# Linear attention and a tanh-shrink MLP on one core: the denominator of batches 3 to 7 taken from TensorE, a DRAM round trip and VectorE to GpSimd and VectorE

## The chip, the cores and the metric

The kernel runs on one core of one Trainium2 chip. The metric is the device time of one execution in microseconds (us), the median of three: 287.32 before (287.25 to 287.70). The profile is of one execution more, with its own time.

## The reference, cut to what matters

```python
# q, k, v: [8 batches, 8 heads, 576, 64] f32
phi = lambda x: np.where(x > 0, x, np.exp(x) - 1.0) + 1.0
kv  = einsum('bhsd,bhse->bhde', phi(k), v)
z   = sum(phi(k), axis=2)
num = einsum('bhsd,bhde->bhse', phi(q), kv)
den = einsum('bhsd,bhd->bhs', phi(q), z)[..., None] + 1e-6
x   = (num / den).transpose(0, 2, 1, 3).reshape(4608, 512)
h   = x @ w_in                  # w_in [512, 2048]
out = (h - tanh(h)) @ w_out     # w_out [2048, 512]
```

Each batch gives 576 rows of x; the MLP takes them in nine blocks of 512 rows.

## The kernel before

Everything is in one hand-written order. A loop of nine passes (`for c in range(NC)`, L509) does the MLP on rows 512c to 512c+511. A pass has two halves of 16 slots each. In **layer 1** a slot is one fi of 16: four matmuls (`l1mm`, L366) of w_in with xT, the transposed x in bf16, into bank fi % 6 of PSUM. After every second slot ScalarE takes tanh of two banks (`l1act2`, L372) and VectorE subtracts, which gives gT in bf16 (L373). In **layer 2** a slot is a quarter of one of four output tiles: four matmuls (`l2mm`, L387) into bank 4 or 5. After slots 3, 7, 11 and 15 ScalarE copies the finished tile to osb (`evac`, L396) and SP writes it out (L403). The dictionaries `s1` and `s2` hold what is put in after a slot: the attention of the batches that later passes need. An engine runs its instructions in the order in which they were written, so a waiting one holds all behind it.

Batches 0 and 1 and part of 2 are prepared in their own way at the start. In the steady part, pass c (c >= 1) with n1 = c + 1 and n2 = c + 2 does this:

- Layer 1, slot 0: `gate` (L383), a copy of one element of qT(n1) on GpSimd, which waits for the transposing DMA; behind it, in GpSimd's queue, the loads of k, q and v of batch n2 (L90), cast to bf16 on the way.
- Layer 1, slot 8 (10 in pass 1): `a_den(n1)`. 16 matmuls (L287) of kz and qT give den for 32 x 4 partitions, in which eight heads and four 16-row groups are folded; kz holds kv in its columns 0 to 63 and, in 64 to 95, z times a mask (L199). VectorE adds 1e-6 (L292) and takes the reciprocal (L296). Then `a_spread(n1)`: SP writes rden to DRAM (four DMAs, L316) and reads it back spread over 64 partitions each (two DMAs, L319) as rdb.
- Layer 2, slots 2, 4, 6 and 8: phi of k (two halves) and of q (two halves): the exponential on ScalarE (L129), max and add (L130) and the minimum (L131) on VectorE. After slot 8 SP issues the transposing DMA (L148), which makes qT(n2) from phi(q). Slots 3 and 5: `a_vp` copies v(n2) beside columns of ones (L190), so that the kv matmuls give z too.
- Layer 2, slot 9 (12 in pass 1): `a_num(n1, n2)`: the num matmuls (L228, and L236 for the last 64 rows), the kv matmuls of batch n2 (L177), then VectorE multiplies num by rdb from PSUM into xT (L333 four times, L338 twice), then `kz_copy(n2)` takes z and kv of batch n2 out of banks 6 and 7 (L199, L200).

The row names in the profile are those of this text. The prediction numbers times within a pass from the start of layer 1 (U) and of layer 2 (T). Other rows that it prices by: L159, transposes of phi(q) on TensorE for batches 0 and 1; L163, L244, L525, ScalarE's copies out of PSUM there; L359, a multiplication of VectorE there; L421, a memset on GpSimd; the select of `masks.py:199`, on GpSimd; L503, a sum of eight elements on VectorE. The kv matmuls of pass 1 that belong to batch 2 stand at its layer 1, slot 8.

Of the kernel before, what the change touches and what calls it, by code (L numbers as in the profile page):

```python
# [11 lines left out]
F32 = mybir.dt.float32  # L12
# [6 lines left out]
def kernel(  # L19
# [15 lines left out]
    NF = DF // 128  # L35
    NC = N // 512
    J = S // 64


    const = ctx.enter_context(tc.tile_pool(name="const", bufs=1))  # L40
# [71 lines left out]


    kp_t, qp_t, qT_t, kz_t, rdb_t, rden_t = {}, {}, {}, {}, {}, {}

    def phi_pieces(b, src, store, name, i, parts=0):

# [71 lines left out]
    def a_vp(b, i):  # L189
        nc.vector.tensor_copy(vp[:, i, :, :, 0:64].rearrange("p j h d -> p h j d"), v_b[b % 2][:, 0:2, i])  # L190

    def kv_cols_mm(b, b0, o):
        kz_t[b] = kz_c[b % 2]
        kv_mm(b, lambda rs, h, i, j: vp[rs, i, j, h, :],
              lambda cs, hg, i: ps_all[cs, b0 + hg, o + 66 * i:o + 66 * i + 66])

    def kz_copy(b, b0, o):
        ps = ps_all[:, b0:b0 + 2, o:o + 132].rearrange("p g (i e) -> p g i e", i=2)
        nc.vector.tensor_mul(kz_t[b][:, :, :, 64:96], ps[:, :, :, 64:65].to_broadcast([128, 2, 2, 32]), mask)  # L199
        nc.vector.tensor_copy(kz_t[b][:, :, :, 0:64], ps[:, :, :, 0:64])  # L200


    def b0_z(i):
# [74 lines left out]
    def a_den(b, bank, parts=range(4)):  # L278

        kz, qT = kz_t[b], qT_t[b]  # L280
        ps = ps_all[:, bank, 0:J * 16]
        for t in range(4) if b == 0 else ():
            nc.tensor.matmul(ps[32 * t:32 * t + 32], eps[:, 0:32], one[:, 0:J * 16], start=True, stop=False)
        for n, p in enumerate((0, 2, 1, 3)):
            if n in parts:
                for t in range(4):
                    nc.tensor.matmul(ps[32 * t:32 * t + 32], kz[:, p // 2, p % 2, 64:96],  # L287
                                     qT[:, p % 2, :, p // 2, 16 * t:16 * t + 16],
                                     start=(n == 0 and b > 0), stop=(n == NP - 1))
        if b > 0:  # L290
            den = rpool.tile([128, J * 16], F32, name="den")
            nc.vector.tensor_scalar(den, ps, 1e-6, None, ALU.add)  # L292
        else:
            den = ps
        rden = rpool.tile([128, J * 16], F32, name="rden")
        nc.vector.reciprocal(rden, den)  # L296
        rden_t[b] = rden
# [25 lines left out]

    def a_num(b, nxt):

        rdb = rdb_t[b]
        for i in range(2):
            num_mm(b, i, lambda h: 2 * h + i)
        rest = rest_mm(b, 6, 0)
        if nxt:  # L330
            kv_cols_mm(nxt, 6, 128)
        for n in range(NP):
            nc.vector.tensor_mul(  # L333
                xT[:, n, S * b:S * b + 512].rearrange("p (j t c) -> p j t c", j=8, t=4),
                ps_all[:, n, :].rearrange("p (j t c) -> p j t c", j=8, t=4),
                rdb[:, n, :, 0:8, :].rearrange("p t j c -> p j t c"))
        for h in range(2):
            nc.vector.tensor_mul(  # L338
                xT[:, 2 * h:2 * h + 2, S * b + 512:S * b + 576].rearrange("p a (t c) -> p a t c", t=4),
                rest[h].rearrange("p a (t c) -> p a t c", t=4), rdb[:, 2 * h:2 * h + 2, :, 8, :])  # L340
        if nxt:
            kz_copy(nxt, 6, 128)

    def new_ns(b):

# [34 lines left out]
    def gate(qT):  # L380

        g0 = rpool.tile([1, 1], BF16, name="g0")
        nc.gpsimd.tensor_copy(g0, qT[0:1, 1, J - 1, 1, 63:64])  # L383
# [6 lines left out]
    def evac(c, i, o, f0=0, f1=None):  # L390
        f1 = DM if f1 is None else f1
        osb = opool.tile([128, DM], F32, name="osb")
        if f0:
            nc.vector.tensor_copy(osb[:, f0:f1], o[:, f0:f1])  # L394
        else:
            nc.scalar.copy(osb[:, f0:f1], o[:, f0:f1])  # L396

        last = c == NC - 1 and i == 3
        for half in range(2):
            b, j = divmod(2 * (4 * c + i) + half, J)  # L400
            cuts = [f0, 256, f1] if c == 3 and i < 3 else [f0, f1]
            for a0, a1 in zip(cuts, cuts[1:]):
                (nc.scalar if last and half else nc.sync).dma_start(  # L403
                    out=out[b * S:(b + 1) * S, a0:a1].rearrange("(p j) m -> p j m", j=J)[:, j, :],
                    in_=osb[64 * half:64 * half + 64, a0:a1])
# [103 lines left out]
    for c in range(NC):  # L509
# [4 lines left out]
        if c == 0:  # L514
            sub = {}

            def spread1(h):
                sub["bp"] = a_spread_pe(1, 4, (2 * h, 2 * h + 1))
                for p in (2 * h, 2 * h + 1):
                    a_scale(1, p, sub["ns"], sub["bp"], 144 * (p % 2))  # L520

            def num1():
                ns = sub["ns"] = new_ns(1)
                for h, ps in enumerate(rest_mm(1, 6, 128)):
                    nc.scalar.copy(ns[:, 2 * h:2 * h + 2, 8, :], ps)  # L525
                for i in range(2):
                    b0 = 4 + 2 * i
                    num_mm(1, i, lambda h: b0 + h)
                    nc.scalar.copy(ns[:, i::2, 0:8, :].rearrange("p a j t -> p a (j t)"), ps_all[:, b0:b0 + 2, :])

            s1[11].append(lambda: a_kphi(1, 0))
            s1[13].append(lambda: a_kphi(1, 1))
            s2[3].append(lambda: a_qphi(1, 0))
            s2[4].append(lambda: (a_qphi(1, 1), load_q(2), load_k(2), load_v(2)))
            s2[0].append(prepare)
            s2[7].append(lambda: (a_qT_pe(1, 0, Banks([4, 5])), a_kv(1, 6), a_qT_pe(1, 1, Banks([4, 5]))))
            s2[8].append(lambda: (scale_rest(0, 6, rdb_t[0]), a_den(1, 4), num1(), a_split(1)))
            s2[10].append(lambda: spread1(0))

            qs, ks = [], []  # L540

            def exp2(pieces, src, store, name, i):
                pieces.append(phi_pieces(2, src, store, name, i))
                pieces[i][0]()

            def rest2(f):
                f[1]()
                f[2]()

            s2[11].append(lambda: exp2(qs, q_t, qp_t, "qp", 0))  # L550
            s2[12].append(lambda: (spread1(1), exp2(qs, q_t, qp_t, "qp", 1), rest2(qs[0])))
            s2[13].append(lambda: (exp2(ks, k_t, kp_t, "kp", 0), rest2(qs[1]), a_qT_dma(2)))
            s2[14].append(lambda: rest2(ks[0]))
        elif n1 < B:
            if c == 1:
                s1[8].append(lambda: (kv_cols_mm(2, 6, 0), kz_copy(2, 6, 0)))
            s1[10 if c == 1 else 8].append(lambda: (a_den(n1, 6), a_spread(n1)))
            s2[12 if c == 1 else 9].append(lambda: a_num(n1, n2 if n2 < B else 0))
        if c == 1:
            s1[1].append(lambda: a_kphi(2, 1))  # L560
            s1[3].append(lambda: (a_vp(2, 0), a_vp(2, 1)))
        if c >= 1 and n2 < B:

            s1[0].append(lambda: (gate(qT_t[n1]), load_k(n2), load_q(n2), load_v(n2)))
            d = 2
            s2[d].append(lambda: a_kphi(n2, 0))
            s2[d + 2].append(lambda: a_kphi(n2, 1))
            s2[d + 4].append(lambda: a_qphi(n2, 0))
            s2[d + 6].append(lambda: (a_qphi(n2, 1), a_qT_dma(n2)))
            for i in range(2):  # L570
                s2[d + 1 + 2 * i].append(lambda i=i: a_vp(n2, i))
        if c == 0:

            first = Banks([4, 5, 6, 7, 0, 1, 2, 3])
            hs = [ps_all[:, n, :] for n in range(4)]
            order = [((0, 0), (0, 1)), ((2, 0), (2, 1), (0, 2), (0, 3), (2, 2), (2, 3)),
                     [(p, fi) for p in (1, 3) for fi in range(4)]]
            seen = [0] * 4
            for n, part_ in enumerate(order):
                if n == 1:  # L580
                    open2()
                for x in range(2 if n == 0 else 0):
                    for p, fi in part_:
                        nc.tensor.matmul(hs[fi][:, 256 * x:256 * x + 256], w_in_sb[:, p, fi * 128:(fi + 1) * 128],
                                         xT[:, p, 256 * x:256 * x + 256], start=(x == 0), stop=False)
                        seen[fi] = 1
                for p, fi in part_ if n else ():
                    l1mm(c, fi, hs[fi], p, seen[fi])
                    seen[fi] += 1
            for fi in range(4):  # L590
                l1act(fi, hs[fi], gT)
# [74 lines left out]
```

## Time and profile before

| | |
|---|---|
| median of three runs | 287.32 us |
| profiled execution, its own time | 287.78 us |
| its span, first to last instruction | 286.0 us |
| mean granted TensorE clock | 0.998 |
| layer 1 of passes 2 to 6, each | 14.28 to 14.29 us |
| layer 1 of pass 7 | 13.81 us |
| transposing DMA, issue to landing, passes 1 to 4 | 6.86, 5.26, 5.19, 4.07 us |
| loads of k, q, v, issue to landing | 6.6, 8.6, 11.1 us |

"Busy" is the time in which an engine ran instructions. PE is TensorE, PEld its weight loads, DVE is VectorE, ACT is ScalarE, POOL is GpSimd, SP only issues DMAs. The chain that ended last is followed back from the last instruction, at each step to what released it; its pieces in order of time give the start, the length and the line. The rows by line give an operation's shape, count, mean duration, and how long its engine was idle just before it and for whom. The transposing DMA's issue is read on SP's timeline, its landing from the gate copy that waits for it.

### The profile page before, as it was taken

What the parts mean: (1) busy time and instruction counts of PE and PEld (TensorE: products, weight loads), DVE (VectorE), ACT (ScalarE), POOL (GpSimd) and SP (SyncE); (2) the same over time, 40 slices, a digit from 0 to 9 for tenths busy, and PEclk for the clock granted to TensorE, in tenths of its full rate; (3) what the DMA queues carried; (4) which work ended last, traced back from release to release, by engine and by line L of the source; (5) the groups of instructions that cost most, each with busy time, mean ns of one, the idle gap of its engine ahead of it and who ended that gap; (6) DMA issues with size and microseconds to landing.
All of it is one profiled execution on the core that took longest, in us unless ns stands there. A gap on an engine that the chain in (4) does not pass through costs nothing.

```text
span 286.0 us, 5195 instructions
## 1 busy us (share of the span) xinstructions
PE 276.8 (97%) x2127; PEld 130.8 (46%) x2155; DVE 171.3 (60%) x271; ACT 139.6 (49%) x167; POOL 30.0 (10%) x50
## 2 busy tenths in 40 slices
PE   8889999999999999999999999999999999999995
PEld 3544464444444444445444544444444444444443
DVE  3749977997558782877277727874680467006600
ACT  4848557857335643564355625661551155126411
POOL 8642030120030003000300030000000000000000
PEclk9999999999999999999999999999999999999999
DMA  6999999997979668955996679656126210230032
GB/s 98 197 206 213 208 207 208 233 179 147 235 148 207 162 102 151 222 127 132 147 208 148 145 142 216 148 126 138 39 75 138 68 37 0 52 82 16 0 76 73
DMA packets 39496, 38.99 MB, mean 136 GB/s; under 512 B 16368, under 2 KB 34608, under 8 KB 38704
## 3 DMA queue, kind: packets, MB, share of 16 engines
q0 software_dynamic: 17488, 18.35, 39.5%
q1 hardware_dynamic: 21824, 20.17, 30.8%
q8 instruction: 17, 0.28, 0.4%
q10 hardware_dynamic: 160, 0.13, 0.1%
q14 instruction: 7, 0.06, 0.1%
HBM read 43.91 MB, written 9.55 MB: 187 GB/s over the span
## 4 chain that ended last, share of the span: by engine, by line
PE 93%; DMA 2%; issue 1%; POOL 1%; DVE 1%; DVEq 0%; POOLq 0%
PE ps_all L366 43%; PE ps_all L387 42%; DMA v<-in_v_dram 2%; PE ps_all L177 2%; PE ps_all L228 1%; PE ps_all L622 1%; PE ps_all L287 1%; PE ps_all L251 1%; POOL kraw L87 1%; DVE xT L255 0%; POOL qraw L87 0%; PE ps_all L159 0%; DVE rden L296 0%; PE ps_all L236 0%; PE ps_all L354 0%
## 5 line engine op out<-in xcount | busy, mean ns | idle before, releaser
L366 PE MATMUL ps_all<-xT,w_in_sb 128*128 128x512 bf16 x559 | 125.4, 379 | 1.2 <-issue 0.5
L387 PE MATMUL ps_all<-w_out_sb,gT 128*128 128x512 bf16 x547 | 122.2, 379 | 1.3 <-issue 1.0
L373 DVE TENSOR_TENSOR gT<-ps_all,th 128x1024 bf16<-128x1024 f32 x64 | 77.8, 1217 | 66.7 <-ACT th L372 66.7
L372 ACT ACTIVATE th<-ps_all 128x1024 f32<-128x1024 f32 x64 | 65.5, 1023 | 50.1 <-PE ps_all L366 50.1
L366 PEld LDWEIGHTS <-w_in_sb 128*128 128x128 bf16 x574 | 55.4, 98 | 67.1 <-issue 0.6
L387 PEld LDWEIGHTS <-gT 128*128 128x128 bf16 x560 | 54.1, 98 | 64.4 <-issue 0.2
L396 ACT COPY osb<-ps_all 128x512 f32<-128x512 f32 (+1 forms) x36 | 20.8, 582 | 74.0 <-PE ps_all L387 49.0
L129 ACT ACTIVATE e<-qraw 128x1152 bf16<-128x1152 bf16 x16 | 18.5, 1160 | 8.4 <-DMA qraw<-in_q_dram 8.4
L333 DVE TENSOR_TENSOR xT<-ps_all,rdb 128x512 bf16<-128x512 f32 x24 | 14.9, 681 | 9.1 <-PE ps_all L228 6.7
L129 ACT ACTIVATE e<-kraw 128x1152 bf16<-128x1152 bf16 x15 | 17.4, 1161 | 0.4 <-DMA kraw<-in_k_dram 0.4
L131 DVE TENSOR_TENSOR qp<-e,r 128x1152 bf16<-128x1152 bf16 x16 | 12.1, 758 | 6.0 <-ACT e L129 5.1
L131 DVE TENSOR_TENSOR kp<-e,r 128x1152 bf16<-128x1152 bf16 x15 | 11.4, 758 | 5.9 <-ACT e L129 4.9
L383 POOL COPY g<-qT 1x1 bf16<-1x1 bf16 x5 | 0.9, 177 | 115.1 <-DMA qT<-qp 115.1
L378 DVE TENSOR_TENSOR gT<-ps_all,th 128x512 bf16<-128x512 f32 x16 | 10.3, 685 | 2.6 <-ACT th L377 2.0
L377 ACT ACTIVATE th<-ps_all 128x512 f32<-128x512 f32 x16 | 9.2, 598 | 4.9 <-PE ps_all L366 3.7
L449 PE MATMUL ps_all<-zero 128*128 128x512 bf16 x29 | 8.7, 460 | 1.2 <-DVE zero L408 1.2
L130 DVE TENSOR_SCALAR r<-qraw 128x1152 bf16<-128x1152 bf16 x16 | 7.5, 468 | 3.0 <-DMA qraw<-in_q_dram 3.0
L296 DVE RECIPROCAL rden<-den 128x144 f32<-128x144 f32 x7 | 7.4, 1053 | 0.2
L394 DVE COPY osb<-ps_all 128x128 f32<-128x128 f32 x1 | 0.3, 290 | 11.6 <-PE ps_all L622 11.6
L130 DVE TENSOR_SCALAR r<-kraw 128x1152 bf16<-128x1152 bf16 x15 | 6.8, 450 | 0.0
L90 POOL DMA_DIRECT2D qraw<-in_q_dram x7 | 5.2, 749 | 13.7 <-DVE r L130 13.0
L177 PEld LDWEIGHTS <-kp 64*64 64x64 bf16 x504 | 5.5, 105 | 0.6 <-DVE vp L190 0.4
(83 smaller groups left out, 111.9 us busy)
## 6 DMA issues: line engine op xcount, KB each, us to landing
out_dram<-osb SPq DMA_DIRECT2D x64, 128.0 KB
rdb<-ds SPq DMA_DIRECT2D x12, 576.0 KB
kraw<-in_k_dram POOLq DMA_DIRECT2D x7, 576.0 KB, 6.6
qraw<-in_q_dram POOLq DMA_DIRECT2D x7, 576.0 KB, 8.6
v<-in_v_dram POOLq DMA_DIRECT2D x7, 576.0 KB, 11.1
w_in_sb<-in_moe_w_in_dram POOLq DMA_DIRECT2D x3, 512.0 KB, 13.4
w_out_sb<-in_moe_w_out_dram POOLq DMA_DIRECT2D x3, 512.0 KB, 19.4
out_dram<-osb SPq DMA_DIRECT2D x12, 64.0 KB
```

Of the source, the lines that this page charges most:

```text
L129: return (lambda: nc.scalar.activation(e, x, AF.Exp), lambda: nc.vector.tensor_scalar(r, x, 0.0, 1.0, ALU.max, ALU.add), lambda: nc.vector ...
L130: lambda: nc.vector.tensor_scalar(r, x, 0.0, 1.0, ALU.max, ALU.add),
L131: lambda: nc.vector.tensor_tensor(y, e, r, ALU.min))
L177: nc.tensor.matmul(ps_of(cs, hg, i), kp[rs, i, j, h, :], v_of(rs, h, i, j), start=(j == 0), stop=(j == J - 1))
L333: nc.vector.tensor_mul(xT[:, n, S * b:S * b + 512].rearrange("p (j t c) -> p j t c", j=8, t=4), ps_all[:, n, :].rearrange("p (j t c) -> p ...
L366: nc.tensor.matmul(h, w_in_sb[:, p, fi * 128:(fi + 1) * 128], xT[:, p, c * 512:(c + 1) * 512], start=(n == 0), stop=(n == NP - 1))
L372: nc.scalar.activation(th, h, AF.Tanh)
L373: nc.vector.tensor_sub(gT[:, fi:fi + 2, :], h, th)
L377: nc.scalar.activation(th, h, AF.Tanh)
L378: nc.vector.tensor_sub(gT[:, fi, :], h, th)
L387: nc.tensor.matmul(o, gT[:, fi, i * 128:(i + 1) * 128], w_out_sb[:, fi, :], start=(fi == 0), stop=(fi == NF - 1))
L396: nc.scalar.copy(osb[:, f0:f1], o[:, f0:f1])
```

## The change

For batches 3 to 7 (`QS = 3`) phi(q) is divided by den before it is transposed, so that num comes out divided.

- `kz_copy` no longer makes the masked z for them; VectorE copies z from PSUM into zr, repeated 64 times along the free axis (bf16). It now stands ahead of the copies into xT, also in pass 1, where batch 2's own multiplications (`num_scale`) come behind it.
- `q_zb`, two slots after a_num: two matmuls of zr with the identity turn z into a row that is the same on all partitions; ScalarE copies it to zb.
- `q_prod`: GpSimd multiplies phi(q) by zb in two halves of 1152 elements, in f32 (the buffers of rdb are used for the products).
- `q_den`: VectorE sums 64 elements at a time, four instructions of 576 elements. Two stand after layer 2's slot 15, two in layer 1 of the next pass, after slots 3 and 5; for batch 3 all stand in layer 1 of pass 2, after slots 2, 5 and 7.
- `q_scale`, after slot 7 (9 in pass 2): VectorE adds 1e-6 and takes the reciprocal of 36 elements; GpSimd multiplies phi(q) by it in place, two halves; then SP issues the transposing DMA.
- `a_den` and `a_spread` are gone for these batches; in `a_num` VectorE copies one half of num into xT and ScalarE the other.
- The loads of batch c + 3 are issued after layer 2's slot 9 of pass c, without the gate; only pass 1 keeps its gate and its loads of batch 3 in layer 1.
- In pass 3 only the first two output tiles are written in half rows.

```diff
+    QS = 3
...
     def kz_copy(b, b0, o):
...
+        if b < QS:
+            nc.vector.tensor_mul(kz_t[b][:, :, :, 64:96], ps[:, :, :, 64:65].to_broadcast([128, 2, 2, 32]), mask)
+        else:
+            zr_t[b] = rpool.tile([128, 2, 2, 64], BF16, name="zr")
+            nc.vector.tensor_copy(zr_t[b].rearrange("p i g t -> p g i t"),
+                                  ps[:, :, :, 64:65].to_broadcast([128, 2, 2, 64]))
         nc.vector.tensor_copy(kz_t[b][:, :, :, 0:64], ps[:, :, :, 0:64])
+    def q_zb(b, bank):
+        ps = ps_all[:, bank, 0:256]
+        for i in range(2):
+            nc.tensor.matmul(ps[:, 128 * i:128 * i + 128], zr_t[b][:, i].rearrange("p g t -> p (g t)"), ident,
+                             start=True, stop=True)
+        zb_t[b] = rpool.tile([128, 2, 128], BF16, name="zb")
+        nc.scalar.copy(zb_t[b].rearrange("p i x -> p (i x)"), ps)
+    def q_prod(b):
+        pr_t[b] = rpool.tile([128, 2, J, 2, D], F32, name="pr", tag="rdb")
+        dn_t[b] = rpool.tile([128, 2, J, 2], F32, name="dn")
+        for i in range(2):
+            nc.gpsimd.tensor_mul(pr_t[b][:, i].rearrange("p j h d -> p j (h d)"),
+                                 qp_t[b][:, i].rearrange("p j h d -> p j (h d)"),
+                                 zb_t[b][:, i].unsqueeze(1).to_broadcast([128, J, 128]))
+    def q_den(b, i, h):
+        nc.vector.tensor_reduce(dn_t[b][:, i, :, h], pr_t[b][:, i, :, h, :], mybir.AxisListType.X, ALU.add)
+    def q_scale(b):
+        dn = dn_t[b].rearrange("p i j h -> p (i j h)")
+        nc.vector.tensor_scalar(dn, dn, 1e-6, None, ALU.add)
+        rd = rpool.tile([128, 2, J * 2], F32, name="rd")
+        nc.vector.reciprocal(rd.rearrange("p i x -> p (i x)"), dn)
+        for i in range(2):
+            x = qp_t[b][:, i].rearrange("p j h d -> p (j h) d")
+            nc.gpsimd.tensor_mul(x, x, rd[:, i].unsqueeze(2).to_broadcast([128, J * 2, D]))
+        a_qT_dma(b)
...
     def a_num(b, nxt):
...
+        if nxt >= QS:
+            kz_copy(nxt, 6, 128)
+        if b >= QS:
+            for h, copy in enumerate((nc.vector.tensor_copy, nc.scalar.copy)):
+                copy(xT[:, 2 * h:2 * h + 2, S * b:S * b + 512], ps_all[:, 2 * h:2 * h + 2, :])
+                copy(xT[:, 2 * h:2 * h + 2, S * b + 512:S * b + 576], rest[h])
+        else:
+            num_scale(b, rest)
...
-            cuts = [f0, 256, f1] if c == 3 and i < 3 else [f0, f1]
+            cuts = [f0, 256, f1] if c == 3 and 2 * i + half < 4 else [f0, f1]
...
-            s1[10 if c == 1 else 8].append(lambda: (a_den(n1, 6), a_spread(n1)))
-            s2[12 if c == 1 else 9].append(lambda: a_num(n1, n2 if n2 < B else 0))
+            if n1 < QS:
+                s1[10].append(lambda: (a_den(n1, 6), a_spread(n1)))
+            else:
+                if c == 2:
+                    s1[2].append(lambda: (q_den(n1, 0, 0), q_den(n1, 0, 1)))
+                e = 2 * (c == 2)
+                s1[3 + e].append(lambda: q_den(n1, 1, 0))
+                s1[5 + e].append(lambda: q_den(n1, 1, 1))
+                s1[7 + e].append(lambda: q_scale(n1))
+            m = 12 if c == 1 else 9
+            s2[m].append(lambda: a_num(n1, n2 if n2 < B else 0))
+            if n2 < B:
+                s2[m + 2].append(lambda: (q_zb(n2, 4 if c == 1 else 7), q_prod(n2)))
+                if c > 1:
+                    s2[15].append(lambda: (q_den(n2, 0, 0), q_den(n2, 0, 1)))
...
-            s1[0].append(lambda: (gate(qT_t[n1]), load_k(n2), load_q(n2), load_v(n2)))
...
-            s2[d + 6].append(lambda: (a_qphi(n2, 1), a_qT_dma(n2)))
+            s2[d + 6].append(lambda: a_qphi(n2, 1))
...
+            if n2 + 1 < B:
+                s2[9].append(lambda: (load_k(n2 + 1), load_q(n2 + 1), load_v(n2 + 1)))
```

More of the change, by code (lines that the diff above doesn't have):

```diff
@@ L114 @@
     kp_t, qp_t, qT_t, kz_t, rdb_t, rden_t = {}, {}, {}, {}, {}, {}
+    zr_t, zb_t, pr_t, dn_t = {}, {}, {}, {}
     def phi_pieces(b, src, store, name, i, parts=0):
@@ L198, in kz_copy @@
         ps = ps_all[:, b0:b0 + 2, o:o + 132].rearrange("p g (i e) -> p g i e", i=2)
-        nc.vector.tensor_mul(kz_t[b][:, :, :, 64:96], ps[:, :, :, 64:65].to_broadcast([128, 2, 2, 32]), mask)
-        nc.vector.tensor_copy(kz_t[b][:, :, :, 0:64], ps[:, :, :, 0:64])
+        if b < QS:
[4 more added lines that the diff above has]
+                                  ps[:, :, :, 64:65].to_broadcast([128, 2, 2, 64]))
+        nc.vector.tensor_copy(kz_t[b][:, :, :, 0:64], ps[:, :, :, 0:64])
+    def q_zb(b, bank):
[23 more added lines that the diff above has]
+        a_qT_dma(b)
     def b0_z(i):
@@ L324, in a_num @@
     def a_num(b, nxt):
-        rdb = rdb_t[b]
         for i in range(2):
@@ L331, in a_num, with num_scale @@
             kv_cols_mm(nxt, 6, 128)
+        if nxt >= QS:
[6 more added lines that the diff above has]
+            num_scale(b, rest)
+    def num_scale(b, rest):
+        rdb = rdb_t[b]
         for n in range(NP):
@@ L340, in a_num @@
                 rest[h].rearrange("p a (t c) -> p a t c", t=4), rdb[:, 2 * h:2 * h + 2, :, 8, :])
-        if nxt:
-            kz_copy(nxt, 6, 128)
     def new_ns(b):
@@ L561 @@
             s1[3].append(lambda: (a_vp(2, 0), a_vp(2, 1)))
+            s1[0].append(lambda: (gate(qT_t[n1]), load_k(n2), load_q(n2), load_v(n2)))
         if c >= 1 and n2 < B:
-            s1[0].append(lambda: (gate(qT_t[n1]), load_k(n2), load_q(n2), load_v(n2)))
             d = 2
```

## The prediction

> **What bounds the kernel now.** I read the busy shares first, then the chain that ended last, then its pieces in order of time, then the rows by line.
>
> ```profile
> PE 276.8 (97%) x2127; PEld 130.8 (46%) x2155; DVE 171.3 (60%) x271; ACT 139.6 (49%) x167; POOL 30.0 (10%) x50
> PEclk9999999999999999999999999999999999999999
> PE 93%; DMA 2%; issue 1%; POOL 1%; DVE 1%; DVEq 0%; POOLq 0%
> ```
>
> TensorE is busy 97% of the span, with nine tenths or more of its clock granted in every slice, and is 93% of the chain; from pass 2 on nothing else stands in that chain but small "issue" gaps. So the time changes only by work put on or taken off TensorE, and by any new wait that makes it stand. VectorE and GpSimd have room on average; whether they have it at the right moment is the question. The chain in order of time (start, length, what), for pass 3 and the last but one, pass 7:
>
> ```profile
> 139.50 5.61 PE ps_all L366 x26
> 145.17 2.11 PE ps_all L366 x9
> 147.28 0.36 PE ps_all L287 x16
> 147.64 5.29 PE ps_all L366 x24
> 152.98 0.81 PE ps_all L366 x3
> 153.79 8.63 PE ps_all L387 x40
> ...
> 227.28 5.61 PE ps_all L366 x26
> 232.94 8.15 PE ps_all L366 x37
> 241.09 2.59 PE ps_all L387 x12
> ```
>
> Layer 1 of pass 3 runs from 139.50 to 153.79: 14.29 us. Pass 7 has the same 64 matmuls and no den: 227.28 to 241.09, 13.81. So the 16 den matmuls of L287 cost 0.48, not the 0.36 of their own piece: changing to them and back costs the rest. Passes 2, 4, 5 and 6 give 14.28 in the same way. A slot (4 matmuls) is 13.81/16 = 0.863 us, in layer 1 and layer 2 alike.
>
> **TensorE, part by part.** Removed: five dens (batches 3 to 7) at 0.47: 2.35 us. Added: five times two matmuls of 128x128 (`q_zb`). Nine matmuls of that shape, the transposes at L159, take 0.50 and 0.61 in the chain, so two are 0.11 to 0.14. The change to another kind of work may cost a gap: 0.16 ("issue") stands behind the kv matmuls in most passes. Bounds 0.11 to 0.30; I take 0.20, five times: 1.0. Net 1.35 off; with the bounds 0.85 to 1.80. The num and kv matmuls stay as they are.
>
> All else must stay off TensorE's path. I check each new wait, in times from the start of layer 2 (T) or layer 1 (U) of a pass.
>
> **`q_zb` waits for VectorE and ScalarE.** It stands behind slot 11. a_num starts at T 8.6; its matmuls and kv end near T 10.1, and two slots later it is T 11.8. Before it VectorE must do zr (in the place of L199; 256 elements as in L200, 0.41) and kz (0.41), from T 10.1: done at T 10.9. ScalarE must have read bank 7: its half of the xT copies is 1024 and 128 elements, L244 1.01 and L525 0.27, from T 9.3: done at T 10.6. So about 0.9 us of cover; gone, each lost us is paid five times, by all of layer 2 queued behind.
>
> **VectorE in layer 1.** Removed per batch: den 0.30 and reciprocal 1.05. Added: four sums of 576 f32 elements. The trace has no such sum: a sum over 8 elements takes 0.16 (L503), a two-source operation on 576 f32 0.75 (L359); these are the bounds, and I take 0.70, near the upper one, since the element count sets it. Then an addition and a reciprocal on 36 elements: 0.4 (a quarter of the 144-element work, plus a little; at most 1.35). Two sums come ahead of the first gT (L373), when VectorE idles: in before it waits 5.3 us there. The other two and the scale each stand behind a gT. gT takes 1.22 of each 1.73; one sum makes a gT at most 0.3 late. TensorE needs a pair of banks again six slots after filling it, that is 5.2 us after the fill begins; tanh and gT end 4.0 after it, which leaves 1.2. With sums in between 0.8 is left, in pass 2, where both first sums fall behind the first gT, about 0.3. Cost nothing; at the 0.75 bound still nothing, or 0.1 once.
>
> **VectorE in layer 2.** Four multiplications (L333, 0.68) and two (L338, 0.28) become a copy of 1024 (L373's size, at most 1.22) and one of 128: earlier, not later. Pass 1 is different: batch 2 keeps its multiplications, but kz(3) now goes ahead of them. They start at 78.6 instead of 77.1, at 0.6 each, and the last of the four ends at 81.1; pass 2 needs it at 80.7 plus five matmuls, 81.8. Hidden by 0.7.
>
> **GpSimd and the transposing DMA, the long chain.** The change puts four two-input multiplications of 1152 elements per batch on GpSimd. No row has one. Below: a memset of the same 1152 (L421) 1.08. Above: the select on 128 elements takes 0.287, nine times that is 2.58; if two inputs were read one after the other, twice: 5.2. I take 2.6, the row nearest in kind, and call its price p.
>
> Products: zb is copied behind the osb copy of slot 11, by T 12.9 (0.37, between L525's 0.27 and L396's 0.58). GpSimd is free: the loads now put into its queue ahead (0.75 each) wait for phi(q)'s end, T 8.7, and are issued by T 10.2. Products end at T 15.5 and T 18.1; the sums that need them are due at T 15.2 (idle VectorE) and T 21. Covered until p is about 4.5.
>
> Scaling: rd is ready at U 10.1 (behind gT of fi 7) and two multiplications end at U 15.3. Then SP issues the transposing DMA; it landed 4.07, 5.19 and 5.26 us after issue in passes 4, 3 and 2 (issue on SP's timeline to the gate copy at L383), and 6.86 in pass 1. With 4.1 to 5.3 qT is there at U 19.5 to 20.7, and num needs it at U 13.8 + 8.6 = 22.4: cover 1.7 to 2.9, until p is 3.5 to 4.0. In pass 2 all is two slots later: rd at 92.7, GpSimd done at 97.9, landed at 102.1 to 103.3; num is due at 103.1. This is the thinnest place: cover 1.0, or short by 0.2. I take the shorter landing: in before the transpose follows two output copies, and in pass 3 six more follow it; now it comes some 12 us after the last output copy was issued. On SP the next output copies queue behind it; they are due at T 3.5 or later and osb has five buffers.
>
> **The loads.** In before the gate (L383) holds them until qT has landed; 11.1 us later v is in. Now they are issued 4 us before layer 1 and land about U 6 to 8, long before the next phi, and before the transpose at U 15.4. Also 30 DMAs of rden (four at L316 and two of 576 KB at L319 per batch) leave SP's queue; batch 2 keeps its six. Neither is on the chain: nothing gained.
>
> The Trainium skill speaks against this placing: "GPSIMD Engine Reference", section "Elementwise — side-by-side cycle accounting", gives two-input work about 2.6 cycles per element at 1.2 GHz. By that page 1152 elements are an estimated 2.5 us plus its dispatch, and the sum would be the same as with my row; no run here has shown it yet. "SBUF — State Buffer", section "Who interferes with whom", says that a VectorE instruction with two SBUF inputs, or in a two-port mode, and a GpSimd instruction lock each other out for a whole instruction. By that rule the second multiplication of pass 2 (to 97.9) would hold back phi(k)'s L130, due at 96.9, by 1.0 us; VectorE waits 0.88 and 0.74 for ScalarE's exponentials in that stretch, so it would cost nothing or a few tenths.
>
> **The sum.** The profiled execution took 287.78: span 286.0 and 1.78 around it. 287.78 - 2.35 + 1.0 = 286.43. It lies 0.46 above the median 287.32, so on the median: 285.97, said as **286.0**.
>
> **Rivals.**
> A, the pass 2 transpose is late: everything as above, but landing takes 5.3 to 6.9, or p is 3.3. TensorE stands 0.2 to 1.7 once, in the middle 1.0: 287.0. For it: cover 1.0 at best. Against: no output copies beside it.
> B, the gaps eat it: q_zb with two gaps and its waits costs 0.4 rather than 0.2, and 0.3 of the den comes back at num; five times 0.4: about 287.2, the change doing nothing. For it: den's 0.48 was one quarter gaps. Against: two matmuls for 16.
> C, slower: GpSimd is the bound. From p = 3.1 in pass 2 and p = 4.0 in passes 3 to 6 qT is late, by two us for each us of p. At p = 4.5: 2 x 4.5 - 6.3 = 2.7 once, and 2 x 4.5 - 8.1 = 0.9 four times: 6.3 - 1.35 = 5.0 slower, 292.3; at the bound of 5.2, 4.1 + 4 x 2.3 = 13.3, 299.3. It decides against the change from p = 3.8 (1.3 in pass 2 alone). For it: no row shows such a multiplication, and VectorE works beside it. Against: the select at 2.24 ns per element.
>
> **How the numbers follow.** Forecast 0.66, A 0.14, B 0.08, C 0.12. The forecast alone spans 287.32 - 1.80 - 0.1 to 287.32 - 0.85 + 0.1: 285.4 to 286.6. A goes to 287.7, and C begins there; the range 285.2 to 288.0 leaves out most of C and little else. About 0.2% (0.57 us) is what a measurement of this kernel can tell from no change: faster is below 286.75, slower above 287.9. Faster: forecast 0.66 and the better part of A: 0.71. Same: rest of A and B: 0.17. Slower: 0.12.
>
> **What would show it.** Layer 1 of passes 2 to 6 at 13.8 in the chain, not 14.29; two matmuls in layer 2 at 0.2 together with their gap; no wait of num on the DMA of qT. GpSimd's rows near 2.6. Wrong if: num waits for qT in pass 2 (A) or in all passes (C), gT waits for sums, or layer 2 grows by more than 0.3.

## The result and the profile after

The changed kernel takes 286.64 us (286.28 to 286.92), the kernel before 287.70 (287.25 to 288.18), nine runs of each taken side by side: 0.9964 of the time before, interval 0.9953 to 0.9974, or 1.06 us less. The profiled execution took 286.75: span 285.0 and 1.77 around it. Against the profiled execution before that is 1.03 less.

Busy shares, granted clock and the chain that ended last, from the page of the kernel after:

```profile
PE 278.0 (98%) x2085; PEld 130.7 (46%) x2085; DVE 174.1 (61%) x271; ACT 147.4 (52%) x182; POOL 74.2 (26%) x66
PEclk9999999999999999999999999999999999999998
PE 85%; DMA 11%; POOL 2%; issue 0%; DVE 0%; POOLq 0%
```

TensorE still sets the time. GpSimd went from 30.0 to 74.2 busy us, and none of it is in the chain after the start. The 11% of DMA are the first loads: the chain is followed back through them here, where before it ran through the first matmuls; layer 1 of pass 1 begins at 50.33, before at 50.22. The chain in order of time, for the pass that the prediction shows at 139.50 (it calls it pass 3; counted by the loop's `c` it is pass 4) and for pass 7:

```profile
139.00 13.81 PE ps_all L414 x64
152.81 8.63 PE ps_all L435 x40
161.44 0.56 PE ps_all L267 x8
162.00 0.06 PE ps_all L275 x8
162.06 0.64 PE ps_all L179 x72
162.70 1.83 PE ps_all L435 x8
164.54 0.11 PE ps_all L214 x2
164.65 3.45 PE ps_all L435 x16
```

```profile
225.53 13.81 PE ps_all L414 x64
239.35 13.81 PE ps_all L435 x64
253.16 13.81 PE ps_all L414 x64
266.97 10.36 PE ps_all L435 x48
277.33 3.51 PE ps_all L684 x32
```

Lines 366 and 387 of before are 414 and 435 here. Layer 1 is one piece of 64 matmuls, 13.81 long, in passes 2 to 6 (14.28 to 14.29 before). Layer 2 of that pass runs from 152.81 to 168.10, 15.29 us, with q_zb (L214) in it; before it took 15.21. Layer 1 of pass 7 begins at 225.53 instead of 227.28: 1.75 earlier. The last matmul, too, ends 1.74 earlier (277.33 + 3.51 = 280.84; before 279.08 + 3.51 = 282.59). But the span became only 1.0 shorter: behind the last matmul there are now 4.15 us where there were 3.44. So 0.7 us were lost after all the arithmetic of TensorE was done.

The new operations, from the rows by line (operation, shape, count, busy time, mean ns of one, then idle time ahead):

```profile
L238 POOL TENSOR_TENSOR qp<-qp,rd 128x1152 bf16<-128x1152 bf16 x10 | 21.0, 2117 | 39.1 <-issue 23.6
L224 POOL TENSOR_TENSOR pr<-qp,zb 128x1152 f32<-128x1152 bf16 x10 | 23.5, 2361 | 24.0 <-ACT zb L217 21.6
L229 DVE TENSOR_REDUCE dn<-pr 128x9 f32<-128x576 f32 x20 | 14.5, 746 | 12.2 <-POOL pr L224 12.2
```

A product takes 2.36 us, a scaling 2.12, a sum 0.746. TensorE's waits in the kernel after (who waited, for whom, total, times, longest) show what became of the covers:

```profile
PE ps_all L497 <- DVE zero L456: 1.2, 1, 1.2
PE ps_all L290 <- DVE kz L261: 0.6, 1, 0.6
PE ps_all L257 <- DMA v<-in_v_dram: 0.4, 1, 0.4
```

These and three smaller ones belong to the start of the program; num on the DMA of qT, q_zb on zr and a layer-2 matmul on gT are not among them. In the transfers of the last microseconds one thing is new. From the view of the DMAs, 280 to 285 us of the kernel after (queue: packets, MB, share of the engines; then the output writes with KB and us to landing):

```profile
q1 hardware_dynamic: 211, 0.20, 18.0%
q10 hardware_dynamic: 160, 0.13, 8.8%
q14 instruction: 1, 0.01, 0.4%
...
out_dram<-osb ACTq DMA_DIRECT2D x1, 96.0 KB, 2.6
...
out_dram<-osb ACTq DMA_DIRECT2D x1, 32.0 KB, 2.8
```

The same view of the kernel before, 281 to 286 us, has two queues only:

```profile
q1 hardware_dynamic: 305, 0.36, 31.3%
q10 hardware_dynamic: 160, 0.13, 8.1%
```

The packet on q14 is a fetch of 8192 bytes of instructions, begun 1.66 us after the last matmul's end, between the last output writes. The last write lands in 16 parts: 15 of them 2.27 to 2.5 us after the last matmul, one at 3.19. Before, the last of the 16 lands at 2.46.

### The profile page after: what moved, and what is told of

It reads as the page before. It is cut to its first block, busy times and chain, and to the rows that moved or that the text cites. A ratio compares the mean times of both kernels' runs of the same rounds, so it can differ in the third digit from the quotient of the medians.

```text
span 285.0 us, 5076 instructions
## 1 busy us (share of the span) xinstructions
PE 278.0 (98%) x2085; PEld 130.7 (46%) x2085; DVE 174.1 (61%) x271; ACT 147.4 (52%) x182; POOL 74.2 (26%) x66
## 4 chain that ended last, share of the span: by engine, by line
PE 85%; DMA 11%; POOL 2%; issue 0%; DVE 0%; POOLq 0%
PE ps_all L435 40%; PE ps_all L414 39%; DMA v<-in_v_dram 8%; DMA w_in_sb<-in_moe_w_in_dram 3%; PE ps_all L179 2%; PE ps_all L267 1%; PE ps_all L684 1%; POOL kraw L88 1%; POOL v L88 0%; POOL qraw L88 0%; POOL v L469 0%; PE ps_all L275 0%; POOL qraw L91 0%; PE ps_all L326 0%; PE ps_all L161 0%
## 5 line engine op out<-in xcount | busy, mean ns | idle before, releaser
L435 PE MATMUL ps_all<-w_out_sb,gT 128*128 128x512 bf16 x560 | 124.6, 379 | 0.0
L435 PEld LDWEIGHTS <-gT 128*128 128x128 bf16 x560 | 53.8, 98 | 63.3 <-issue 0.2
L238 POOL TENSOR_TENSOR qp<-qp,rd 128x1152 bf16<-128x1152 bf16 x10 | 21.0, 2117 | 39.1 <-issue 23.6
L224 POOL TENSOR_TENSOR pr<-qp,zb 128x1152 f32<-128x1152 bf16 x10 | 23.5, 2361 | 24.0 <-ACT zb L217 21.6
L229 DVE TENSOR_REDUCE dn<-pr 128x9 f32<-128x576 f32 x20 | 14.5, 746 | 12.2 <-POOL pr L224 12.2
L133 DVE TENSOR_TENSOR qp<-e,r 128x1152 bf16<-128x1152 bf16 x16 | 12.1, 759 | 5.5 <-ACT e L131 4.6
L133 DVE TENSOR_TENSOR kp<-e,r 128x1152 bf16<-128x1152 bf16 x15 | 11.4, 759 | 5.5 <-ACT e L131 4.6
L91 POOL DMA_DIRECT2D kraw<-in_k_dram x7 | 5.6, 803 | 28.1 <-ACT e L131 19.8
L497 PE MATMUL ps_all<-zero 128*128 128x512 bf16 x29 | 9.5, 491 | 1.2 <-DVE zero L456 1.2
L374 DVE CAST xT<-ps_all 128x1024 bf16<-128x1024 f32 x5 | 6.1, 1217 | 6.9 <-PE ps_all L275 6.9
L132 DVE TENSOR_SCALAR r<-qraw 128x1152 bf16<-128x1152 bf16 x16 | 7.5, 467 | 3.2 <-DMA qraw<-in_q_dram 3.2
```

Source lines behind the costliest of these rows:

```text
L91: nc.gpsimd.dma_start(out=t.rearrange("q h i j d -> q (h i) (j d)"), in_=x.rearrange("(n q) x -> q n x", n=4))
L133: lambda: nc.vector.tensor_tensor(y, e, r, ALU.min))
L224: nc.gpsimd.tensor_mul(pr_t[b][:, i].rearrange("p j h d -> p j (h d)"), qp_t[b][:, i].rearrange("p j h d -> p j (h d)"), zb_t[b][:, i].uns ...
L229: nc.vector.tensor_reduce(dn_t[b][:, i, :, h], pr_t[b][:, i, :, h, :], mybir.AxisListType.X, ALU.add)
L238: nc.gpsimd.tensor_mul(x, x, rd[:, i].unsqueeze(2).to_broadcast([128, J * 2, D]))
L435: nc.tensor.matmul(o, gT[:, fi, i * 128:(i + 1) * 128], w_out_sb[:, fi, :], start=(fi == 0), stop=(fi == NF - 1))
```

## The experiments

The theory after these traces, **T**: on TensorE the change is what the prediction said, 0.47 less per den and a little more per q_zb, and no wait was added; **S**: the longer end is systematic, not an accident of one execution (N). Against T stood that q_zb and its surroundings cost as much as in rival B, and that the den's removal is worth less than its 0.47 in the kernel's time. The letters are those of the expectations.

### Both kernels again

> The kernel before, once more. Between the last matmul's end and the span's end stood 3.4 us in the profile of before (282.57 to 286.01) and 4.15 in that of after (280.83 to 284.98): of the 1.75 us that TensorE gained the last small writes took 0.7 back. Theory N (the landing of the last writes varies from run to run in either kernel): this tail lies anywhere from 3.3 to 4.3, and the ratio is 1.000 within 0.001. Theory S (the change itself lengthens the tail): the tail is 3.4 again, within 0.1.

Measured: 287.58 us, ratio 0.9998 (0.9988 to 1.0007); last matmul to the end 3.38.

> The changed kernel, once more. Theory N: the tail differs from 4.15 by some tenths, and with five rounds the ratio is near the 0.9940 that TensorE's 1.75 us make. Theory S: the tail is 4.15 within 0.1 and the ratio stays at 0.9964 (1.06 us). In both the layers of passes 2 to 6 are as before in the trace of after: layer 1 13.81, layer 2 15.28.

Measured: 286.84, ratio 0.9971 (0.9961 to 0.9982); last matmul to the end 4.15 again, with the fetch and the one late part at 3.17. S stands, N falls.

### Without the dens alone

```diff
+    dsrc = const.tile([128, J * 16], F32, name="dsrc")    # 600.0
...
+        if b >= 3:
+            ps = dsrc
         for n, p in enumerate((0, 2, 1, 3)):
-            if n in parts:
+            if n in parts and b < 3:
```

> The kernel before without the den matmuls of batches 3 to 7: VectorE adds and takes the reciprocal of a constant instead, all else is as before (spread through DRAM, multiplications, loads), so the output is another. Theory T: layer 1 of passes 2 to 6 is 13.81 instead of 14.28, in all 2.35 us below the kernel before, ratio 0.9918. Theory D (the changed kernel's gain comes from less DMA traffic and the earlier loads, not from TensorE's den): ratio 0.998 to 1.000.

Measured: 285.48, ratio 0.9921 (0.9909 to 0.9934): 2.27 us less than before. The chain of this kernel in pass 4 (layer 1 is L369, layer 2 is L390):

```profile
138.63 5.61 PE ps_all L369 x26
144.24 0.05 issue
144.29 8.15 PE ps_all L369 x37
152.44 2.59 PE ps_all L390 x12
```

Layer 1 is 138.63 to 152.44, 13.81. The end is 3.40 long, as before. So the dens are worth 0.47 each in the trace, and 0.45 by the time.

### Without q_zb's matmuls

```diff
-        ps = ps_all[:, bank, 0:256]
-        for i in range(2):
-            nc.tensor.matmul(ps[:, 128 * i:128 * i + 128], zr_t[b][:, i].rearrange("p g t -> p (g t)"), ident,
-                             start=True, stop=True)
...
-        nc.scalar.copy(zb_t[b].rearrange("p i x -> p (i x)"), ps)
+        nc.scalar.copy(zb_t[b].rearrange("p i x -> p (i x)"), zr_t[b].rearrange("p i g t -> p (i g t)"))
```

> The changed kernel without the two matmuls of q_zb: ScalarE copies zr itself into zb, so z is not spread over the partitions and the output is another. Theory T (time follows what stands on TensorE, all else is covered): layer 2 of passes 2 to 5 shorter by 0.08 to 0.11, in all 0.45 us below the changed kernel, ratio 0.9948. Theory B (the two matmuls bring gaps and waits): 1.0 to 2.0 us below it, ratio 0.990 to 0.993.

Measured: 286.11, ratio 0.9951 (0.9938 to 0.9963), 0.0020 or 0.57 us under the kernel after. Each of five layers 2 is 0.11 shorter than in the second trace of the kernel after (pass 4: 15.18 against 15.29). q_zb is two matmuls of 0.055 and no gap; rival B's 0.4 is out.

### Which stream fetches at the end

Pass 3's output is cut into fewer pieces in the kernel after, which changes SP's stream of instructions. Theory **F**: the fetch is SP's, and the old cutting moves it away. **G**: it belongs to the stream of VectorE or ScalarE, and a few more instructions there move it.

```diff
-            cuts = [f0, 256, f1] if c == 3 and 2 * i + half < 4 else [f0, f1]
+            cuts = [f0, 256, f1] if c == 3 and i < 3 else [f0, f1]
```

> The changed kernel with pass 3's cut of before (three tiles written in half rows instead of two): two more output copies on SP, nothing else. In the traces of the changed kernel, of its second run and of the one without q_zb an instruction fetch of 8192 bytes falls 1.62 to 1.66 us after the last matmul, among the last small writes, and one of the sixteen parts of the last write lands 0.7 us behind the other fifteen; the kernels before have no such fetch there and a tail of 3.4 us. Theory F (that fetch is SP's own: its instruction stream now crosses a block just there): two more copies move the crossing to an earlier output copy, the tail is 3.4 and the time 0.7 us below the changed kernel, ratio to before 0.994. Theory G (another engine's stream, or something else in the change): tail 4.15 to 4.3, ratio 0.9965.

Measured: 286.94, ratio 0.9980 (0.9972 to 0.9989); the fetch still begins 1.62 us after the last matmul, the end is 4.49 long. F falls.

```diff
+        if c == 7:
+            def tiny():
+                tv = rpool.tile([128, 1], F32, name="tv")
+                ta = rpool.tile([128, 1], F32, name="ta")
+                for _ in range(6):
+                    nc.vector.memset(tv, 0.0)
+                    nc.scalar.copy(ta, zero[:, 0:1])
+            s2[1].append(tiny)
```

> The changed kernel with six tiny instructions more on VectorE and six more on ScalarE in pass 7, where both idle; SP's stream is unchanged. Theory F: the fetch stays where it is, tail 4.15 to 4.3, ratio 0.9965. Theory G in the form that the fetch is VectorE's or ScalarE's: the fetch moves to an earlier time, tail 3.4, ratio 0.994.

Measured: 285.85, ratio 0.9939 (0.9926 to 0.9953). Twelve instructions that do nothing made the kernel 0.7 to 0.9 us faster than the kernel after, by its two ratios (0.9964 and 0.9971). The fetch moved from 282.49 to 268.92, the end is 3.38 long. G stands; of which engine was open. Three more kernels ask that (theory **V** says VectorE's), the first with VectorE's six memsets alone (f_v), the second with ScalarE's six copies alone (f_a), both at the same place, and the third with VectorE's six at the start of the program (f_v0), where they can change nothing at the end but the position in the stream:

```diff
     nc.vector.memset(one, 1.0)
+    tv = const.tile([128, 1], F32, name="tv")
+    for _ in range(6):
+        nc.vector.memset(tv, 0.0)
```

> The changed kernel with six tiny memsets more on VectorE in pass 7; ScalarE is left as it is. With six on each of the two the late fetch of 8192 bytes moved from 1.66 us behind the last matmul to 268.9, and the tail was 3.38. Theory V (it is VectorE's stream that crosses a block at the end; VectorE's last copy starts as the last matmul ends, which fits a fetch at the same distance every time): tail 3.4, time 0.75 us below the changed kernel, ratio to before 0.994. Theory A (ScalarE's): tail 4.15 to 4.3, ratio 0.9965.

Measured: 286.09, ratio 0.9937 (0.9924 to 0.9949); end 3.46, fetch at 269.34.

> The changed kernel with six tiny copies more on ScalarE in pass 7; VectorE is left as it is. Theory V: tail 4.15 to 4.3, ratio 0.9965. Theory A: tail 3.4, ratio 0.994.

Measured: 287.01, ratio 0.9966 (0.9952 to 0.9979); end 4.20, fetch still 1.66 us after the last matmul, one part of the last write at 3.23. (A second fetch, at 285.52, comes after the end: ScalarE's copies did push something, harmlessly.)

> The changed kernel with the same six tiny memsets on VectorE, but at the start, before its first phi. Theory V, with the position in the stream deciding: as with the six in pass 7, tail 3.4, ratio 0.994. If only what runs late counts, or if the stream is ScalarE's: tail 4.15 to 4.3, ratio 0.9965.

Measured: 286.08, ratio 0.9937 (0.9925 to 0.9949); end 3.44, fetch at 242.91.

So it is VectorE's stream, and its length up to the end decides, not what is done near the end. The last transfers of f_v, 280 to 285 us:

```profile
q1 hardware_dynamic: 230, 0.24, 21.8%
q10 hardware_dynamic: 160, 0.13, 8.4%
...
out_dram<-osb ACTq DMA_DIRECT2D x1, 96.0 KB, 2.4
...
out_dram<-osb ACTq DMA_DIRECT2D x1, 32.0 KB, 2.1
```

No q14, and ScalarE's last write lands in 2.1 us instead of 2.8. f_v, f_v0 and f_ctl are the fastest versions here that leave no part of the work out; each beats both kernels.

How the fetch holds up the writes shows in the single packets. Eight traces have the fetch among the last writes. In seven of them (all but the first of the kernel after) exactly ten packets of writes begin behind its end, the first within 0.01 us of it: five of SP's queue, then five of ScalarE's, in each four of 512 bytes and one of 4. That is a sixteenth of each of the last two writes. The last write packet ends 2.34 to 2.49 us after the last matmul, against 2.05 to 2.06 in the six traces without the fetch, and the last part lands at 3.14 to 3.31, against 2.40 to 2.48. So the part waits for the fetch; why its landing is later by 0.7 us and more, where its packets are later by 0.3 to 0.4, is not shown.

### How far the covers reach

To find the edges of the covers I doubled GpSimd's work, first in the scaling, then in the products. **C1** says that this uses up the cover that the prediction worked out; **C3** that GpSimd and VectorE hold each other up as well.

```diff
             nc.gpsimd.tensor_mul(x, x, rd[:, i].unsqueeze(2).to_broadcast([128, J * 2, D]))
+            nc.gpsimd.tensor_mul(x, x, rd[:, i].unsqueeze(2).to_broadcast([128, J * 2, D]))
```

> The changed kernel with each of q_scale's multiplications done twice (phi(q) is divided by den twice, so the output is another). In the trace of after they take 2.10 each, the transposing DMA lands 3.9 after its issue. Theory C1 (the cover of the chain rd, GpSimd, DMA, num is 2.4 us in pass 2 and about 4 in passes 3 to 6, as read from the trace of after): 4.2 us more make num 1.9 us late in pass 2 and 0 to 0.3 late in each of passes 3 to 6, in all 1.9 to 3.1 above the changed kernel. Theory C2 (this chain is not what num waits for next; slack elsewhere): no stall, time as the changed kernel. Theory C3 (GpSimd and VectorE lock each other out in the phi that now runs beside it): over 4 us above, with VectorE's L132 or L133 late.

Measured: 292.20, ratio 1.0153 (1.0119 to 1.0188), about 5.3 us more than the kernel after by the ratios, above what C1 gave. But its four executions go from 290.33, with a granted clock of 1.0, to 293.32, with 0.988, and the profiled one is the slowest. In it passes 3 to 6 are 0.2 to 0.4 longer each, and pass 2 takes 33.36 instead of 29.11. TensorE's longest wait, VectorE from 97.9 to 103.2 and GpSimd beside it:

```profile
PE ps_all L268 <- DMA qT<-qp: 3.3, 4, 2.7
```

```profile
97.94 0.46 DVE L132 TENSOR_SCALAR r<-kraw 128x1152 bf16<-128x1152 bf16 x1
98.50 2.48 DVE L133 TENSOR_TENSOR kp<-e,r 128x1152 bf16<-128x1152 bf16 x1
100.91 2.37 DVE L192 COPY vp<-v 128x1152 bf16<-128x1152 bf16 x1
```

```profile
98.04 2.33 POOL L238 TENSOR_TENSOR qp<-qp,rd 128x1152 bf16<-128x1152 bf16 x1
100.45 2.51 POOL L239 TENSOR_TENSOR qp<-qp,rd 128x1152 bf16<-128x1152 bf16 x1
```

In pass 2 num waits 2.7 us for the transposing DMA: rival C's place. Beside the scaling, L133 takes 2.48 us (0.759 in its row in the kernel after) and the copy L192 2.37 (0.46 in the kernel after). L133 ends at 100.98, 0.61 after GpSimd's first, and L192 at 103.28, 0.32 after the second, a little less than each needs by itself: as C3 says, VectorE stood until GpSimd's whole instruction had ended. GpSimd's own two took 2.33 and 2.51 instead of 2.12, which makes the transposing DMA, and num, 0.6 later. VectorE's own delay cost nothing here: phi(k) was done at 104.51, and num began at 107.00.

The rest of pass 2's 4.25 is TensorE's clock. The chain behind num's first matmuls, and the clock by slices of 7.3 us:

```profile
107.68 0.90 PE ps_all L179 x68
108.58 3.10 PE ps_all L436 x8
```

```profile
PEclk9979999999999988999999999999999999999999
```

The kv matmuls take 0.90 where they took 0.64, and the eight of layer 2 take 3.10 where they took 1.83. The granted clock is 0.5 from 107.72 to 111.13 and full again behind that. The wait of 2.66, with 0.26 and 1.27 for the slow matmuls, makes 4.19 of the 4.25. A second such stretch, from 15.56 to 18.97, falls ahead of pass 1, which begins at 51.52 instead of 50.33; the kernel after has none before its last matmul. The execution with the full clock is 3.5 to 3.7 above the kernel after; C1's upper end (3.1) and the 0.6 of GpSimd would make that up, but it has no trace. Whether the wait brings on the half clock was not tested.

```diff
             nc.gpsimd.tensor_mul(pr_t[b][:, i].rearrange("p j h d -> p j (h d)"),
                                  qp_t[b][:, i].rearrange("p j h d -> p j (h d)"),
                                  zb_t[b][:, i].unsqueeze(1).to_broadcast([128, J, 128]))
+            nc.gpsimd.tensor_mul(pr_t[b][:, i].rearrange("p j h d -> p j (h d)"),
+                                 qp_t[b][:, i].rearrange("p j h d -> p j (h d)"),
+                                 zb_t[b][:, i].unsqueeze(1).to_broadcast([128, J, 128]))
```

> The changed kernel with each of q_prod's multiplications done twice (the same result written again, the second time over the first). 2.36 each becomes 4.7 per half. The prediction called this covered until 4.5 per half. Theory C1: the first two sums end a gT 0.8 late, which the banks allow, the later ones make a gT late by 0.2 to 0.7 beyond the banks' slack; 0.5 to 3 us above the changed kernel, with TensorE waiting in layer 1 for gT. Theory C2: no stall, within 0.4 of the changed kernel.

Measured: 289.93, ratio 1.0078 (1.0064 to 1.0093), 3.1 to 3.3 us more than the kernel after by the ratios. From its waits:

```profile
PE ps_all L417 <- DVE gT L424: 2.0, 6, 0.5
```

Layer 1 (L417) waits for banks that gT (L424) has not emptied, because the sums ahead of gT in VectorE's queue wait for GpSimd. Passes 3 to 6 lose 0.55 to 0.60 each, pass 2 1.06. No wait on the DMA of qT shows here.

### The loads back behind layer 1's first slot

```diff
+        elif c > 1 and n2 < B:
+            s1[0].append(lambda: (load_k(n2), load_q(n2), load_v(n2)))
...
-            if n2 + 1 < B:
-                s2[9].append(lambda: (load_k(n2 + 1), load_q(n2 + 1), load_v(n2 + 1)))
```

> The changed kernel with the loads of batches 4 to 7 issued after slot 0 of layer 1, as before the change, but without the gate: half a pass later than in the changed kernel, behind the products in GpSimd's queue. Theory T (loads are not on the chain in either place): v lands about 12 us after issue, near the end of layer 1, just before a_vp needs it and before or beside the transposing DMA; the time is that of the changed kernel within 0.3, ratio 0.9955 to 0.9975, tail 4.15. Theory L (the earlier loads are a part that the change needs): ScalarE's exponentials or VectorE's a_vp wait for the loads, or the transposing DMA lands later than 5 us after issue and num waits: 0.5 us and more above the changed kernel.

Measured: 286.66, ratio 0.9960 (0.9948 to 0.9972), end 4.12 with the fetch. The place of the loads is worth nothing that can be measured here.

## Why the prediction was right in direction and short in size

The direction, the mechanism and the range held, the size in part by luck: two terms were off, with opposite signs, TensorE's gain by 0.4 and the end by 0.7. The gain was 1.06 where 1.35 was forecast; the time forecast is lower still by 0.3 because it starts from the three-run median of 287.32, and later medians of the kernel before are 287.58 to 287.89. Step by step:

- **Dens, 0.47 each.** Right: 0.47 in each of five passes, 2.36 together, and 2.27 by the time of the kernel without them.
- **q_zb, 0.20 each.** Too dear: "I take 0.20" put a gap behind the pair that isn't there. Layer 2 grew by 0.06 to 0.09 in four of the five passes and by 0.19 in pass 3 (0.12 of which stays without the pair; why is not shown); the pair itself is 0.11, the lower bound, by the kernel without it. The gap of 0.16 "behind the kv matmuls" that bounded it is a misreading: it stands where the trace lacks the record of a matmul. Six slots, 24 matmuls, follow the kv matmuls; the kernel before shows 23 behind its gap, and 0.16 + 5.13 = 5.29:

  ```profile
  163.71 0.16 issue
  163.87 5.13 PE ps_all L387 x23
  ```

  The kernel after, in its first trace, has all 24 and no gap, in 1.83 + 3.45 = 5.28 beside the pair's 0.11. Its second trace has seven instead of the first's "162.70 1.83 PE ps_all L435 x8", and the 0.16 ahead of them; 0.16 + 1.67 is 1.83 again:

  ```profile
  162.75 1.67 PE ps_all L435 x7
  ```

  From the start of pass 1 to the last matmul TensorE takes 1.81 to 1.85 less in the two pairs of traces, where 1.35 was forecast; pass 1 itself begins 0.1 to 0.3 later in those of the kernel after, and anywhere from 49.8 to 50.5 in other traces whose start is the same.
- **The end, taken as fixed.** This is the step that went wrong. The sum ran from TensorE's path to the total as if what follows the last matmul were a constant. It grew by 0.7: the change moved VectorE's stream of instructions so that one of its fetches fell among the last writes. 1.74 - 0.71 = 1.03, the whole difference of the two profiled executions. That moving the fetch brings the 0.7 back is shown three times, and the packets show that one part in each of the last two writes begins only behind the fetch; that these share one of the 16 DMA engines with it fits this, but the profile does not name a packet's engine. The Trainium skill, "Runtime: NRT & Kernel Launch", section "Instruction fetch mechanics", has each sequencer fetch its stream in blocks by a DMA queue of its own and calls the cost mostly hidden; the cost agrees with six of the seven fetches on q14 here, which no wait in the chain follows, and not with the one among the last writes, which cost 0.7 us. A queue for each engine does not show in the profile: the fetch that VectorE's memsets moved and the one that ScalarE's copies brought, at 285.52, are both on q14.
- **q_zb's wait, cover 0.9.** Held, with less: ScalarE's 128-element copy stood 0.55 for `kz` and ended at 105.6 in pass 2, q_zb came at 106.2: 0.6 left. The prediction had it go ahead at once.
- **VectorE's sums, 0.70 each.** 0.746, and no gT came late by enough for TensorE to wait.
- **GpSimd, p = 2.6.** 2.36 for a product and 2.12 for a scaling. For the products, "Covered until p is about 4.5" was well placed: at twice 2.36 = 4.72 each pass from 3 to 6 loses half a microsecond. For the scaling, "until p is 3.5 to 4.0" goes with 2 x 4.24 - 8.1 = 0.4 at twice 2.12, by the formula of rival C; measured 0.2 to 0.4.
- **Pass 1, "Hidden by 0.7".** Held: the last of the four multiplications ends at 81.23, and layer 1 of pass 2 is 13.81.
- **Pass 2, "cover 1.0, or short by 0.2".** Held by more: rd at 92.4, scaled at 96.76, and with the DMA's 3.9 us qT is there at 100.7, 2.4 before num at 103.1. Of the 1.4 more than "1.0", 1.0 is the cheaper p (twice 2.6 - 2.12), the rest an earlier rd and a landing of 3.9 instead of 4.1. Rival A had no ground: the shorter landing was the right choice, though the reason given for it is doubtful (last section).
- **The two rules of the skill.** GpSimd's rows, 2.36 and 2.12 us, are a little under the 2.5 us estimated from "GPSIMD Engine Reference", section "Elementwise — side-by-side cycle accounting". The mutual lock of "SBUF — State Buffer", section "Who interferes with whom", did not bite in the kernel after, where phi(k)'s L132 begins at 96.74, just as the scaling ends (96.76); in the kernel with doubled scaling it did, with 2.48 for 0.76.
- **Loads: nothing gained.** Right, by the kernel with the loads put back.

Rival C did not come, since p is 2.12 for the scaling; with the scaling doubled its formula for the threshold held in passes 3 to 6. In pass 2, 2 x 4.24 - 6.3 = 2.2, and num waited 2.66, with GpSimd 0.6 slower beside VectorE; the pass lost 4.25, because the granted clock was 0.5 for 3.4 us behind the wait. C had neither the lock nor the clock.

What stays open: why VectorE's fetch comes at 269.34 with six memsets in pass 7 and at 242.91 with six at the start, and why the last one on q14 came at 244.60 in the kernel before; the profile does not number the instructions in a stream (it records 271 of VectorE in both kernels).

## What to carry to other kernels

Where one engine bounds the kernel, its pieces in the chain give the price of removed and added work to a tenth of a microsecond; count the matmuls beside a gap before pricing it, since a missing record looks like one. Then look past the last matmul: set the time from its end to the span's end against that of the kernel before, since a difference there has nothing to do with the work moved, and a few instructions in a stream may be worth as much as the change. A cover is worth checking by doubling the work that it hides: that shows whether the threshold was right, and what else it brings on the way, here a lock between two engines and a stretch of half clock.

## What the runs showed of the hardware that was not expected

- An instruction fetch of 8192 bytes among the last output writes made one of the 16 parts of a write land 0.7 us later and more (3.14 to 3.31 us after the last matmul in eight traces, against 2.40 to 2.48 in six without it). Six memsets of one column on VectorE, in the last passes or at the program's start, took it away: 0.9937 of the time before, where the kernel after has 0.9964.
- Beside a two-input multiplication on GpSimd, a two-input minimum on VectorE went from 0.76 to 2.48 us and a plain bf16 copy from 0.46 to 2.37, while GpSimd's own went from 2.12 to 2.33 and 2.51.
- Behind a wait of 2.66 us TensorE's granted clock was 0.5 for 3.41 us, beginning 0.7 us after the first matmul; eight matmuls took 3.10 us instead of 1.83 (kernel with the scaling doubled, one execution).
- The transposing DMA of 128 x 2304 elements landed 3.9 us after its issue in each of the five of the change, with no output copies just ahead of it. In the kernel before it took 6.81, 5.14 and 5.07 us in passes 1 to 3, but 3.96 and 3.98 in passes 4 and 5, with four output copies issued just ahead in each: such copies alone do not make it late.
